# Sparse attention and two feed-forward layers: two inner slices per unit, value low halves off VectorE, one reciprocal per two pairs

## The chip, the cores and the metric

The kernel runs on one core of one Trainium2 chip. The metric is the device time of one execution in microseconds (us), the median of the runs. Five engines work side by side, each through its own instructions in order: TensorE (PE; its weight loads are listed as PEld), VectorE (DVE), ScalarE (ACT), GpSimd (POOL) and SyncE (SP, which only issues transfers here). An instruction that waits holds up all that stands behind it on its engine.

## What is computed

```python
def _attn_ref(q, k, v):                       # (4, 8, 576, 64) each
    scores = (1 / np.sqrt(D)) * np.matmul(q, k.transpose(0, 1, 3, 2))
    kth = np.partition(scores, -32, axis=-1)[..., -32:-31]
    scores = np.where(scores >= kth, scores, -1e9)
    attn = np.exp(scores - np.max(scores, axis=-1, keepdims=True))
    attn = attn / (np.sum(attn, axis=-1, keepdims=True) + 1e-9)
    return np.matmul(attn, v)
def _moe_ref(x, w_in, w_out):                 # 2304 tokens, 512 -> 2048 -> 512
    r = np.maximum(x @ w_in, 0.0)
    return (r * r) @ w_out
def _moe2_ref(x, w_skip, w_gate, w1, w2):     # 8 experts, 512 -> 1024 -> 512
    # tokens with x @ w_skip > 0 go to the expert with the largest logit:
    # x + probability * (relu(x @ w1[e]) @ w2[e]); the others stay as they are
```

All arrays are float32. The output of the attention is the input of the first feed-forward layer, and that one's output is the input of the second.

## The kernel before

Products are made in float16 with split numbers: a value is held as a high half and a low half, and three of the four products are summed. So nearly every operand is scaled, rounded to its high half, and subtracted from itself to get the low half.

**Attention.** The 18,432 rows of scores (4 batches, 8 heads, 576 rows) make 144 tiles of 128 rows by 576 columns. They are taken two at a time, in 72 ticks (`j`; `a` and `b` are the two tiles of a tick). In a tick PE makes the next pair's scores in PSUM (`qk`, tile `pS`, which has one buffer), ACT evacuates them to SBUF (`evac_s`, tile `s`), and DVE folds them into pairwise maxima and minima (`tree`, L360), finds the 32 largest values by four rounds of MAX and MATCH_REPLACE (`top32`, L379, L382) and writes a mask (`mask`, L406). ACT makes the exponentials (L401), POOL multiplies them by the mask (L415), ACT rounds them to the high half and sums the rows (`high`, L430, into `l`), POOL subtracts the low half (`low`, L435), and SP transposes both by DMA. Three ticks later PE multiplies by the values (`av`, L458), DVE has made the reciprocal of the row sums (`rinv`, L419), and ACT scales the result by it (`xout`, L476).

**Preparing q, k and v.** Raw pieces come by DMA into one of three `raw` buffers. For q and k, ACT makes the high half and a scaled copy in place, and POOL subtracts (`low_pool`). For the 32 value pieces (`vh`, 128 by 320) ACT makes the high half (L242) and DVE the low half in one instruction, with a sum for a later range check (L245, `low_dve`), placed behind `top32` and ahead of the next pair's `tree`.

**First feed-forward layer, interleaved.** When the tokens of a group are ready (a group is one token tile of 128, or two of them), `add_units` queues 16 units for it, one per slice of 128 of the inner width. A unit is: 12 matmuls into PSUM (`mm1`, L535), three ACT passes (`act1`: relu `r` L543, square `g` L545, square in float16 `gh` L547), one POOL subtraction (`g_low`, L556), and 3 matmuls per token tile (`mm2`, L568). Fourteen groups have one tile, two have two, so there are 224 units of 128 columns and 32 of 256. Each tick runs 4.4 units' worth of 128 columns, as far as units are there; the transposed tokens of a one-tile group lie in tile `xl` (shown under its tag as `xb` or `xl`), which has two buffers. What is left runs in a loop after the last tick, in which the logits, the routing (`route`), the scatters of token ids by POOL (`scatter_ids`, L837, while fewer than `DRAIN` units are left) and the split of the first 16 expert weight chunks (`next_chunk`: ACT L875, DVE L880 or POOL L877 and L878) stand among the units. The chunks' buffers lie where the attention's tiles were, so their first loads come after the last transposition of tokens.

**Second layer.** The tokens of each expert are gathered, and its blocks run one after the other.

The code gives the order of each engine only in part: a scheduler places the instructions, by priorities and dependences, when the kernel is built. The changed code therefore also stands in another order where its text is the same.

## Time and profile before

| | us |
|---|---|
| three runs | 1027.30, 1023.33, 1030.25 (median 1027.3) |
| the profiled execution | 1023.65 |
| its span, first to last instruction | 1021.8 |
| VectorE busy in the span | 845.7 (83%) |
| TensorE busy | 779.8 (76%) |
| GpSimd busy | 767.4 (75%) |
| ScalarE busy | 759.8 (74%) |

Busy times are unions over the whole span, and the span has stages that are limited by different things: the 72 ticks (to about 741 us), the loop over the units that are left (to about 833 us), and the second layer.

### The profile page before, as it was taken

The page shows a single profiled execution, that of the slowest core. Times are in us where ns is not written, and L with a number is a line of the kernel's source. Part 1 is how long each engine was busy: PE and PEld are TensorE (multiplying, and loading weights), DVE is VectorE, ACT ScalarE, POOL GpSimd, SP SyncE. Part 2 cuts the span into 40 slices and gives each one's busy share as a digit, 9 for nine tenths or more (in the row PEclk, how much of TensorE's full clock was granted, in tenths as well). Part 3 has the DMA queues.
Part 4 walks back from the last instruction along what each step waited for, and adds up shares of the span by engine and source line. Part 5 has one row for each costly group of instructions (what it writes and reads, how often), then busy time and mean ns, then how long its engine had stood idle before and what let it go on. Part 6 is the DMA issues. An engine that isn't in the chain of part 4 may idle for free. (4 is left out here: it accounts for less than half of the span.)

```text
span 1021.8 us, 25759 instructions
## 1 busy us (share of the span) xinstructions
PE 779.8 (76%) x9036; PEld 592.5 (58%) x9036; DVE 845.7 (83%) x2279; ACT 759.8 (74%) x2117; POOL 767.4 (75%) x783
## 2 busy tenths in 40 slices
PE   0123337989879979989969999999997958688852
PEld 0122226767667757667657777767775746565631
DVE  4999999999999999999989999999908634535631
ACT  7777676899988998888779989999866642544620
POOL 4576777899879898888879988899955875744850
PEclk9999999999999999999979999999998978898876
DMA  9675554668675475565475676565537508653500
GB/s 286 174 189 152 141 126 78 103 137 156 118 161 111 94 150 94 108 130 119 100 137 121 138 138 130 116 117 90 96 64 269 208 27 326 214 177 113 177 15 10
DMA packets 257023, 138.16 MB, mean 135 GB/s; under 512 B 215348, under 2 KB 238260, under 8 KB 256848
## 3 DMA queue, kind: packets, MB, share of 16 engines
q1 hardware_dynamic: 253568, 132.16, 55.7%
q0 software_dynamic: 3280, 3.80, 1.2%
q8 instruction: 94, 1.54, 0.6%
q14 instruction: 81, 0.66, 0.2%
HBM read 76.92 MB, written 7.37 MB: 82 GB/s over the span
## 5 line engine op out<-in xcount | busy, mean ns | idle before, releaser
L379 DVE MAX8 m<-tr 128x8 f32<-128x288 f32 (+1 forms) x576 | 275.8, 517 | 0.0
L435 POOL TENSOR_TENSOR phl<-e,phl 128x576 f16<-128x576 f32 x144 | 190.6, 1328 | 33.2 <-ACT phl L430 29.0
L415 POOL TENSOR_TENSOR e<-e,mk 128x576 f32<-128x576 f32 x144 | 196.0, 1371 | 21.9 <-DVE mk L406 21.9
L568 PE MATMUL px<-woh,gh 128*128 128x512 f16 x576 | 189.3, 382 | 15.9 <-POOL gh L556 10.8
L382 DVE MATCH_REPLACE8 tr<-m,tr 128x288 f32<-128x288 f32 x432 | 186.8, 437 | 0.0
L535 PEld LDWEIGHTS <-wih 128*128 128x128 f16 x2048 | 143.2, 101 | 55.4 <-issue 23.6
L535 PE MATMUL ph<-xb,wih 128*128 128x128 f16 (+1 forms) x1792 | 156.6, 231 | 21.0 <-DMA xb<-xhl 9.5
L458 PE MATMUL misc<-vh,pt 128*128 128x64 f16 (+1 forms) x2400 | 119.3, 198 | 63.7 <-ACT xn L476 33.7
L556 POOL TENSOR_TENSOR gh<-g,gh 128x128 f16<-128x128 f32 (+1 forms) x256 | 130.2, 515 | 41.1 <-ACT gh L547 27.4
L458 PEld LDWEIGHTS <-pt 128*128 128x128 f16 (+1 forms) x2400 | 100.8, 100 | 85.3 <-issue 53.2
L568 PEld LDWEIGHTS <-gh 128*128 128x128 f16 x864 | 77.5, 100 | 86.0 <-POOL gh L556 21.1
L360 DVE SCALAR_TENSOR_TENSOR tr<-pS,s 128x576 f32<-128x576 f32 x144 | 102.1, 750 | 14.8 <-ACT s L332 10.8
L401 ACT ACTIVATE e<-s,nm 128x576 f32<-128x576 f32 x144 | 111.0, 772 | 1.4 <-POOL phl L435 0.7
L568 PE MATMUL px<-wol,gh 128*128 128x512 f16 x288 | 109.7, 382 | 0.0
L430 ACT ACTIVATE phl<-e 128x577 f16<-128x577 f32 x144 | 98.0, 681 | 2.8 <-POOL e L415 2.8
L543 ACT ACTIVATE r<-ph 128x128 f32<-128x128 f32 (+1 forms) x256 | 70.3, 287 | 37.9 <-PE ph L535 36.8
L535 PE MATMUL ph<-xb,wil 128*128 128x128 f16 (+1 forms) x896 | 97.4, 230 | 0.0
L326 PE MATMUL pS<-kh,ql 128*128 128x192 f16 x576 | 67.2, 273 | 38.9 <-DMA kh<-lp 26.1
L406 DVE TENSOR_SCALAR mk<-s,m 128x576 f16<-128x576 f32 x144 | 93.3, 688 | 0.0
L545 ACT ACTIVATE g<-r 128x128 f32<-128x128 f32 (+1 forms) x256 | 82.7, 324 | 7.1 <-POOL gh L556 3.4
L332 ACT ACTIVATE s<-pS 128x1152 f32<-128x1152 f32 x72 | 80.3, 1116 | 3.7 <-PE pS L326 3.4
L547 ACT ACTIVATE gh<-r 128x128 f16<-128x128 f32 (+1 forms) x256 | 80.7, 320 | 1.3 <-PE px L568 1.0
(229 smaller groups left out, 1585.6 us busy)
## 6 DMA issues: line engine op xcount, KB each, us to landing
wraw<-in_w SPq DMA_DIRECT2D x64, 512.0 KB, 5.4
wol<-in_w_in SPq DMA_DIRECT2D x16, 512.0 KB, 4.9
raw<-in_qm SPq DMA_DIRECT2D x48, 128.0 KB, 2.8
w<-in_w_out SPq DMA_DIRECT2D x10, 512.0 KB, 3.7
raw<-in_vd SPq DMA_DIRECT2D x32, 160.0 KB, 2.8
raw<-in_kd SPq DMA_DIRECT2D x16, 288.0 KB, 3.5
out<-x SPq DMA_DIRECT2D x16, 256.0 KB, 2.6
wol<-in_w_out SPq DMA_DIRECT2D x6, 512.0 KB, 3.7
```

The costliest lines, as they stand in the source:

```text
L360: last = nc.vector.scalar_tensor_tensor(out=R2[:, :, n * 288:n * 288 + 288].rearrange("p k (c x) -> p k c x", c=3), in0=near, scalar=2.0 * ...
L379: return both(lambda k: nc.vector.max(m[k][:, 8 * r:8 * r + 8], x[k][:, :n]))
L382: both(lambda k: nc.vector.match_replace(out=dst[k][:, :n], in_to_replace=m[k][:, 8 * r:8 * r + 8], in_values=src[k][:, :n], imm_value=NEG))
L401: nc.scalar.activation(e[:, :S], st[i]["s"], AF.Exp, scale=0.125, bias=st[i]["nm"])
L406: nc.vector.tensor_scalar(out=t, in0=st[i]["s"], scalar1=st[i]["m"][:, 31:32], scalar2=None, op0=ALU.is_ge)
L415: nc.gpsimd.tensor_mul(e[:, :S], e[:, :S], st[i]["mk"])
L430: nc.scalar.activation(h[:, 0, :S + 1], st[i]["e"], AF.Copy, accum_out=st[i]["l"][:, 0:1])
L435: nc.gpsimd.tensor_sub(h[:, 1, :S], st[i]["e"][:, :S], h[:, 0, :S])
L458: nc.tensor.matmul(ps[:, a, :], lhsT=pt[:rows, 5 * low + c, :], rhs=vh[:rows, c, part * D:(part + 1) * D], start=(n == 0), stop=(n == len( ...
L535: nc.tensor.matmul(ph, lhsT=wt[:, d, u["f"] * 128:(u["f"] + 1) * 128], rhs=x[:, :, c0 + d, :], start=(n == 0), stop=(n == 11))
L556: g_last[0] = nc.gpsimd.tensor_sub(u["gh"][:, 1], u["g"], u["gh"][:, 0]).ins
L568: nc.tensor.matmul(px, lhsT=gh[:, part, t * 128:(t + 1) * 128], rhs=w[:, f, :], start=(f == 0 and n == 0), stop=(f == 15 and n == 2))
```

## The change

It has three parts.

1. A unit of a one-tile group takes two slices of the inner width: two accumulations of 12 matmuls side by side in one PSUM tile, then ACT and POOL instructions of 256 columns, then two times 3 matmuls. Such a group has 8 units and not 16. PE's matmuls stay as they were, shape by shape. `DRAIN` counts units, and is halved.
2. The low half of a value piece is made as those of q and k are: ACT scales the raw piece in place (one more pass), and POOL subtracts in its queue of low halves. The range check on those sums goes, with its four small DVE instructions.
3. The row sums of two pairs stand in one tile of 2 by 4, and every second tick makes the reciprocals of all four tiles. The reciprocal of the earlier pair is made where it was; for the later pair it is made a tick earlier relative to its use, and so it needs the row sums of the tick just before.

```diff
-DRAIN = 12
+DRAIN = 6
...
-            slot = (v_["b"] * 4 + v_["pr"]) * 2 + hd
-            low_dve.append(lambda: nc.vector.scalar_tensor_tensor(
-                out=vh[:, :, D:], in0=t3, scalar=2.0 ** V_EXP, in1=vh[:, :, 0:D],
-                op0=ALU.mult, op1=ALU.subtract, accum_out=v_low[:, slot:slot + 1]))
+            nc.scalar.activation(t, t, AF.Copy, scale=2.0 ** V_EXP)
+            low_pool.append(lambda: nc.gpsimd.tensor_sub(vh[:, :, D:], t3, vh[:, :, 0:D]))
...
-        l = apool.tile([128, 2, 2], F32, name="l", bufs=6)
+        if a % 4 == 0:
+            l4[:] = [apool.tile([128, 2, 4], F32, name="l", bufs=4)]
+        l = l4[0]
         for k in range(2):
-            st[a + k].update(m=m[:, k], nm=nm[:, k:k + 1], l=l[:, :, k])
+            st[a + k].update(m=m[:, k], nm=nm[:, k:k + 1], l=l[:, :, a % 4 + k])
...
     def rinv(a):
         l = st[a]["pair"][2]
-        nc.vector.reciprocal(l[:, 1], l[:, 0])
+        if a % 4 == 0:
+            nc.vector.reciprocal(l[:, 1], l[:, 0])
...
-            for f in range(16):
-                units.append(dict(gr=gr, f=f, n=128 * len(gr[1])))
+            step = 2 // len(gr[1])
+            for f in range(0, 16, step):
+                units.append(dict(gr=gr, fs=range(f, f + step), n=256))
...
-        ph = psum.tile([128, 256], F32, name="ph", bufs=2)[:, :u["n"]]
-        n = 0
-        for wt, c0 in ((wih, 0), (wih, 4), (wil, 0)):
-            for d in range(4):
-                nc.tensor.matmul(ph, lhsT=wt[:, d, u["f"] * 128:(u["f"] + 1) * 128], rhs=x[:, :, c0 + d, :],
-                                 start=(n == 0), stop=(n == 11))
-                n += 1
+        ph = psum.tile([128, 256], F32, name="ph", bufs=2)
+        for i, f in enumerate(u["fs"]):
+            w = 256 // len(u["fs"])
+            n = 0
+            for wt, c0 in ((wih, 0), (wih, 4), (wil, 0)):
+                for d in range(4):
+                    nc.tensor.matmul(ph[:, i * w:i * w + w], lhsT=wt[:, d, f * 128:(f + 1) * 128], rhs=x[:, :, c0 + d, :],
+                                     start=(n == 0), stop=(n == 11))
+                    n += 1
...
-            for job in low_dve:
-                with tc.issue_after(tail):
-                    tail = job().ins
-            low_dve.clear()
...
-    vl = rpool.tile([128, 4 * H], F32, name="vl")
-    nc.vector.tensor_tensor(out=vl, in0=v_low, in1=v_low, op=ALU.mult)
-    check(7, vl, 9216.0 ** 2, ALU.is_le)
```

Three places in the order show what moves. The first is DVE around a tick late in the attention (`m` the 32 values found, `tr` the folded scores, `mk` the mask). Before:

```order
L379 MAX m_10699<-tr 128x8 x2
L419 RECIPROCAL l<-l 128x2
L382 MATCH_REPLACE tr<-m_10699,tr 128x288 x2
L379 MAX m_10699<-tr 128x8 x2
L245 SCALAR_TENSOR_TENSOR vh,v_low<-raw,vh 128x5x64
L360 SCALAR_TENSOR_TENSOR tr<-pS,s 128x2x288 x2
L406 TENSOR_SCALAR mk<-s,m_10699 128x576 x2
```

After:

```order
L380 MAX m_10166<-tr 128x8 x2
L421 RECIPROCAL l<-l 128x4
L383 MATCH_REPLACE tr<-m_10166,tr 128x288 x2
L380 MAX m_10166<-tr 128x8 x2
L361 SCALAR_TENSOR_TENSOR tr<-pS,s 128x2x288 x2
L407 TENSOR_SCALAR mk<-s,m_10166 128x576 x2
```

The value's low half is gone from between the last round of MAX and the next `tree`; the reciprocal is twice as wide, and the next tick has none.

The second is ACT where the last tile of tokens is split (`xhl`), after the last tick (`r`, `g`, `gh` are the three passes of a unit, `xn` the attention's output). Before:

```order
L476 ACTIVATE xn<-misc,l 128x64 x2
L492 ACTIVATE xhl,x_sq<-xn 128x512
L493 ACTIVATE xhl<-xn 128x512
L547 ACTIVATE gh<-r 128x128 x2
L543 ACTIVATE r<-ph 128x128
L547 ACTIVATE gh<-r 128x128
```

After:

```order
L478 ACTIVATE xn<-misc,l 128x64 x2
L550 ACTIVATE g<-r 128x256
L494 ACTIVATE xhl,x_sq<-xn 128x512
L495 ACTIVATE xhl<-xn 128x512
L552 ACTIVATE gh<-r 128x256
```

The unit passes are twice as wide, and there are fewer of them left: behind the last split of `xhl` ACT still has the `r` pass of 37 units of 128 columns before, and of 15 units of 256, which is 30 of 128, after. Behind the last exponential it is 46 before and 40 after.

The third is POOL at the end of the loop over the units (the scatters of token ids are `table<-ent,sloti`). Before, a stretch of the twelve pairs of a subtraction and a scatter:

```order
L556 TENSOR_TENSOR gh<-g,gh 128x128
L837 DMA table<-ent,sloti 18432x2
L556 TENSOR_TENSOR gh<-g,gh 128x128
L837 DMA table<-ent,sloti 18432x2
L556 TENSOR_TENSOR gh<-g,gh 128x128
```

After, the first of six:

```order
L880 TENSOR_TENSOR w21l<-wraw,w21h 128x1024
L561 TENSOR_TENSOR gh<-g,gh 128x256
L839 DMA table<-ent,sloti 18432x2 x2
L561 TENSOR_TENSOR gh<-g,gh 128x256
L839 DMA table<-ent,sloti 18432x2 x2
```

As many scatters stand ahead of the last unit's subtraction as before, twelve, but two together, and between half as many subtractions.

## Rows read from the trace of the kernel before

**Rows 1.** Busy time by stage: each engine's busy us (instructions), then PEclk, DMA share, GB/s.
```profile
33.00:741.00 708.00, 566.29 (x6840) 434.65 (x6841) 697.36 (x1935) 605.60 (x1776) 598.62 (x623) 0.98 0.62 125
741.00:765.00 24.00, 24.00 (x297) 17.88 (x295) 0.45 (x5) 15.64 (x60) 12.62 (x24) 1.00 0.36 62
765.00:802.00 37.00, 29.61 (x284) 22.13 (x282) 34.13 (x108) 26.67 (x70) 22.12 (x26) 0.91 0.75 268
802.00:833.00 31.00, 26.12 (x252) 18.85 (x249) 8.55 (x31) 13.38 (x49) 26.29 (x33) 0.95 0.26 86
833.00:1022.00 189.00, 129.58 (x1350) 95.71 (x1350) 88.19 (x168) 75.60 (x120) 96.03 (x62) 0.82 0.41 142
```

**Rows 2.** Costliest groups, DVE: count, then busy us, mean ns, idle before.
```profile
L245 DVE SCALAR_TENSOR_TENSOR vh<-raw,vh 128x320 f16<-128x320 f32 x32 | 21.2, 678 | 0.0
L419 DVE RECIPROCAL l<-l 128x2 f32<-128x2 f32 x72 | 10.3, 142 | 3.8 <-ACT phl L430 3.8
L406 DVE TENSOR_SCALAR mk<-s,m 128x576 f16<-128x576 f32 x144 | 93.3, 688 | 0.0
```

**Rows 3.** Timeline of DVE in one tick: start us, us.
```profile
610.94 0.15 DVE L419 RECIPROCAL l<-l 128x2 f32<-128x2 f32 x1
611.01 0.07 DVE L382 MATCH_VALUE_LOAD tr<-m,tr 128x8 f32 x1
...
613.18 0.47 DVE L245 SCALAR_TENSOR_TENSOR vh<-raw,vh 128x320 f16<-128x320 f32 x1
...
613.58 0.75 DVE L360 SCALAR_TENSOR_TENSOR tr<-pS,s 128x576 f32<-128x576 f32 x1
```

**Rows 4.** Timeline of ACT near the same tick.
```profile
603.64 0.19 ACT L430 ACTIVATION_READ_ACCUMULATOR phl<-e 128x1 f32 x1
...
612.06 1.11 ACT L332 ACTIVATE s<-pS 128x1152 f32<-128x1152 f32 x1
```

**Rows 5.** Who waited for whom: us in total, times, longest.
```profile
DVE tr L360 <- ACT s L332: 10.8, 5, 4.3
```

**Rows 6.** Two tiles' instructions: ns min/median/max, first and last start.
```profile
L406 DVE TENSOR_SCALAR mk<-s,m x144: 500/592/1536, 34.2 to 740.0; 128x576 f16<-128x576 f32 x144
L245 DVE SCALAR_TENSOR_TENSOR vh<-raw,vh x32: 461/483/1434, 63.7 to 650.6; 128x320 f16<-128x320 f32 x32
```

**Rows 7.** Groups with shapes kept apart, ACT and POOL.
```profile
L545 ACT ACTIVATE g<-r 128x128 f32<-128x128 f32 x224 | 69.3, 310 | 6.9 <-POOL gh L556 3.4 <-ACT nm L387 0.3
L545 ACT ACTIVATE g<-r 128x256 f32<-128x256 f32 x32 | 13.5, 421 | 0.2
L242 ACT ACTIVATE vh<-raw 128x320 f16<-128x320 f32 x32 | 14.9, 466 | 15.3 <-DMA raw<-in_vd 15.2
L556 POOL TENSOR_TENSOR gh<-g,gh 128x128 f16<-128x128 f32 x224 | 108.1, 489 | 38.8 <-ACT gh L547 25.2 <-ACT g L545 5.5 <-DMA wraw<-in_w 2.2
L556 POOL TENSOR_TENSOR gh<-g,gh 128x256 f16<-128x256 f32 x32 | 22.1, 696 | 2.3 <-ACT gh L547 2.3
L222 POOL TENSOR_TENSOR ql<-raw,ql 128x256 f16<-128x256 f32 x48 | 36.9, 770 | 13.9 <-ACT raw L221 13.8
```

**Rows 8.** Timeline of POOL and SP from the last split to the first expert load.
```profile
755.30 1.16 POOL L494 TENSOR_TENSOR xhl<-xn,xhl 128x512 f16<-128x512 f32 x1 [2.98 <-ACT xhl L493]
...
761.43 1.23 SPq L500 DMA_TRANSPOSE xb<-xhl  x1
...
764.61 0.34 POOL L772 MEMSET blank<- 128x288 int32 x1 [0.94 <-DMA xb<-xhl]
```

**Rows 9.** Timeline of ACT: first and last of the first 16 chunks.
```profile
768.64 1.06 ACT L875 ACTIVATE w10h<-wraw 128x1024 f16<-128x1024 f32 x1 [1.49 <-DMA wraw<-in_w]
...
800.42 1.06 ACT L875 ACTIVATE w21h<-wraw 128x1024 f16<-128x1024 f32 x1
```

**Rows 10.** Timeline of POOL: two scatters, one unit apart.
```profile
817.08 0.99 POOL L837 DMA_INDIRECT table<-ent,sloti  x1 [0.17 <-issue]
818.71 0.99 POOL L837 DMA_INDIRECT table<-ent,sloti  x1 [0.17 <-issue]
```

More of the change, by code (lines that the diff above doesn't have):

```diff
@@ L122, in attention_two_moes @@
     lg_all = const.tile([128, NT, 9], F32, name="lg_all")
-    v_low = const.tile([128, 4 * H], F32, name="v_low")
     w_sq = const.tile([128, 20], F32, name="w_sq")
@@ L208, in new_v @@
         return apool.tile([128, 5, 2 * D], F16, name="vh", bufs=BUFS["v"])
-    low_pool, low_dve = [], []
+    low_pool = []
     def prep_piece(pc):
@@ L343, in attention_two_moes @@
     m6 = [None]
+    l4 = []
     def pair_tiles(a):
@@ L561, in mm2 @@
     def mm2(u):
-        f, gh, gr = u["f"], u["gh"], u["gr"]
-        if f == 0:
-            x2p[gr] = [psum.tile([128, DM], F32, name="px", bufs=2) for _ in gr[1]]
-        for t, px in enumerate(x2p[gr]):
-            n = 0
-            for part, w in ((0, woh), (0, wol), (1, woh)):
-                nc.tensor.matmul(px, lhsT=gh[:, part, t * 128:(t + 1) * 128], rhs=w[:, f, :],
-                                 start=(f == 0 and n == 0), stop=(f == 15 and n == 2))
-                n += 1
+        gh, gr = u["gh"], u["gr"]
+        for i, f in enumerate(u["fs"]):
+            if f == 0:
+                x2p[gr] = [psum.tile([128, DM], F32, name="px", bufs=2) for _ in gr[1]]
+            for t, px in enumerate(x2p[gr]):
+                n = 0
+                for part, w in ((0, woh), (0, wol), (1, woh)):
+                    nc.tensor.matmul(px, lhsT=gh[:, part, (t + i) * 128:(t + i + 1) * 128], rhs=w[:, f, :],
+                                     start=(f == 0 and n == 0), stop=(f == 15 and n == 2))
+                    n += 1
         if f == 15:
@@ L1187, in attention_two_moes @@
     check(6, w_abs, 2.0 ** -97, ALU.is_le)
-    vl = rpool.tile([128, 4 * H], F32, name="vl")
-    nc.vector.tensor_tensor(out=vl, in0=v_low, in1=v_low, op=ALU.mult)
-    check(7, vl, 9216.0 ** 2, ALU.is_le)
-    check(8, m31, 2.0 ** -6, ALU.is_ge)
-    nc.vector.tensor_reduce(out=good[:, 8:9], in_=good[:, 0:9], axis=AX.X, op=ALU.min)
+    check(7, m31, 2.0 ** -6, ALU.is_ge)
+    nc.vector.tensor_reduce(out=good[:, 8:9], in_=good[:, 0:8], axis=AX.X, op=ALU.min)
     cnt_f = rpool.tile([128, 8], F32, name="cnt_f")
```

## The prediction

> **What bounds the kernel now.** I read the stages first, since the four compute engines are all busy 74 to 83% of the span and a sum over it says little. In the 72 ticks, 33 to 741 us, VectorE is busy 697.4 of 708 us, while PE, ACT and POOL have 566, 606 and 599 [rows 1]: the ticks go at DVE's pace, and each microsecond off DVE there is one off the kernel, as long as the others keep up. From 741 to 765 DVE has 0.45 us of work and PE is busy all 24 us: PE works off units that have queued up, while the last pair goes through POOL, DMA, PE and ACT. From 765 to 802 DVE is again the busiest, 34.1 of 37, now with routing and the low halves of expert weights, and the units share ACT with the weight chunks. From 802 to 833 POOL (26.3 of 31) and PE (26.1) are level. The second layer, 189 us, contains nothing that the diff touches, and I move it as a block.
>
> **Part A, DVE in the ticks.** The 32 low halves took 678 ns in the mean [rows 2]. In the tick shown, the instruction took 0.47 us, but the next one began 0.40 us after it [rows 3]; instructions overlap by 0.07 us at their ends. So 32 x (0.678 - 0.07) = 19.5 us leave DVE's queue. The reciprocals read 142 ns [rows 2], but the next instruction begins 0.07 us after one [rows 3]: 36 x 0.07 = 2.5 us. Together 22.0 us. The row of 2 by 4 is not in the trace; by the row of 2 columns I take it as equal, and a size twice that would cost 36 x 0.07 = 2.5 us at the most, so the reciprocals are worth 0 to 2.5.
>
> Not all 22 can be had, since the scores run in a loop beside DVE: `tree` frees the one `pS`, PE makes the next scores, ACT evacuates them, and the next `tree` waits for that. In the tick shown the evacuation ends at 612.06 + 1.11 = 613.17 [rows 4] and `tree` starts at 613.58 [rows 3]. That is 0.41 us of slack, just what the removed instruction took. Five of the 72 trees waited already, 10.8 us in all [rows 5]. ACT gets lighter (below), which helps the loop; PE's blocks between two scores get longer, which hurts it. I take three quarters, **-16.5 us**; the ends are -8 (the loop eats most) and -24 (all of it, and 2 us of the old waits).
>
> The reciprocal's new need is the row sums of the tick before. The sum that the one at 610.94 would need [rows 3] was read at 603.64 + 0.19 = 603.83 [rows 4], 7.1 us ahead. I price that wait at nothing; the cover is those 7 us, and behind it would wait a MATCH_REPLACE and all of DVE's tick.
>
> **What ACT and POOL give and take in the ticks.** 112 pairs of narrow units become 112 wide ones. One ACT pass saves 2 x 310 - 421 = 199 ns per pair [rows 7]; with three passes of about that size, 112 x 3 x 0.199 = 67 us less on ACT, of which some 50 in the ticks. The 32 new passes over 128x320 cost what L242 does on that shape, 466 ns [rows 7], 15 us. POOL saves 112 x (2 x 489 - 696) = 31.6 us [rows 7] and gets 32 subtractions of 128x320. Their price lies between 128x256 at 770 ns [rows 7] and 128x512 at 1160 [rows 8]; in proportion 870, so 27.8 us (24.6 to 37.1). POOL ends 4 us lighter (7 lighter to 5.5 heavier), at about 599 of 708 us before. Neither sets the pace, so none of this enters the sum.
>
> That speaks against a rule of the Trainium skill: GPSIMD Engine Reference, section 4.1, sends elementwise work on two inputs to VectorE because GpSimd is about half as fast. As an estimate from that page, twice the trace's 461 ns is 0.92 us, or 29.5 us for the 32; the rows' 27.8 agree. By the rule taken alone the sum would be 16.5 us worse, without part A.
>
> More serious is that DVE and POOL get into each other's way. A mask takes 500 ns at the least, 688 in the mean, 1536 at the most; the low half 461 to 1434 [rows 2, 6]. The masks lose 144 x 188 = 27 us of DVE's time. A new subtraction could stand in a mask's way: 32 x half of 0.87 = 14 us if every one did. Against that, 112 POOL instructions disappear. I put the balance at zero, and +14 is a rival. In the Trainium skill, SBUF — State Buffer, section "Who interferes with whom", such a stall is an exclusive lock: whichever of the two starts first holds the shared ports for its whole instruction. By that rule the removed low halves also stop delaying POOL; the spread of the rows fits it.
>
> **Part B, from the last tick to the first expert load.** POOL finished the low half of the last tokens at 755.30 + 1.16 = 756.46, but their transposition was issued at 761.43, and what waits for it began at 764.61 [rows 8]. Those 4.97 us are no POOL time. The last tile's tokens need one of the two `xl` buffers; it is free when only 32 units are left to start (16 of this group and 16 of the one ahead). In the order before, 37 units' passes stand behind that split, five too many; after, 30. So the wait goes: **-4.9 us** (0 to -5). Late next is the chain through POOL itself, which is unchanged.
>
> **Part C, units among weight chunks.** Between the first and the 16th chunk on ACT lie 768.64 to 801.48 [rows 9], 32.8 us, with 15 units before and 14 after. DVE has work for 34.1 of the stage's 37 us [rows 1], so no more than 2.9 can go. A wide unit's three passes each may wait behind one more chunk, 1.06 us [rows 9]: 7 x 1.06 = 7.4 at worst. I take **-1** (-3 to +7).
>
> **Part D, the end of the loop.** There POOL alternates one scatter and one subtraction per unit: two scatters stand 818.71 - 817.08 = 1.63 us apart [rows 10]. After, two units cost 2 x 1.63 - 2 x 0.489 + 0.696 = 2.98 against 3.26, six times: 6 x 0.28 = **-1.7** (-4 to +3, since a wide unit takes longer to fill and empty the pipeline). The four check instructions that go stand beside DVE's idle time here: nothing.
>
> **Sum.** -16.5 - 4.9 - 1 - 1.7 = -24.1 us. The profiled execution took 1023.65 and becomes 999.5. It lies 3.65 us below the median of the runs, so for the median I forecast 1027.3 - 24.1 = **1003.2 us**.
>
> **Rivals.** (1) The score loop takes DVE's place: PE's longer blocks stand ahead of the next scores, the evacuation ends later, and part A keeps only a third, -7 us. For it: the 0.41 us of slack, PE at 80% in the ticks. Against: five waits in 72 so far, and the lighter ACT. 1027.3 - 7 - 4.9 - 1 - 1.7 = 1012.7. (2) The same mechanism beyond the break-even, the slower side: `tree` waits in every tick. Over the 59 ticks from 200 us on, in which units run, a mean wait of 24.1 / 59 = 0.41 us in a tick more than I allow eats the whole gain. A unit that is twice as long can cost one subtraction more on POOL before `mm2` lets PE go on, 0.70 us: 1027.3 - 24.1 + 59 x 0.70 = 1044.5. Against: the scores stand between units once a tick, in both orders, and nothing waits for them then but one block. (3) The new subtractions meet the masks: +14, so 1017.2. For it: the 27 us that masks lose now; against: POOL's instructions fall by 80. (4) More comes out of the two loops at the end: fewer hand-overs between PE, ACT and POOL let C and D reach -3 and -4, and ACT's relief lets A reach -22: 1027.3 - 22 - 4.9 - 3 - 4 = 993.4. (5) The reciprocal does wait after all, because ACT runs later: each of 36 would cost what ACT is late beyond 7.1 us. At 0.5 us each, 18 us: 1021.2.
>
> **How the numbers follow.** The forecast has 0.60, (4) 0.14, (1) 0.11, (3) 0.07, (2) 0.05, (5) 0.03. My own bounds around the forecast are 1027.3 - 24 - 5 - 3 - 4 = 991 and 1027.3 - 8 - 3 + 3 + 2 = 1021; all bad ends at once are unlikely, and I cut at the rivals (1) and (3). The range is 989 to 1016: it holds the forecast, (1) and (4), and leaves out (2), (5), most of (3) and some of the forecast's bad ends, together under 0.2. Runs of one kernel here spread over 7 us, so 1%, 10.3 us, is about what can be told from no change. Under 1017 lie nearly all of the forecast, (4), (1) and half of (3): 0.85 for faster by over 1%. Within 1%: 0.09, from the rest of (3), (5) and bad ends. Slower: 0.06, from (2) and what I have not thought of.
>
> **What would show it.** Right for A: the ticks end near 724 us instead of 741, no L245 on DVE, 36 reciprocals, DVE still busy over 98% until then, and waits of `tree` for `s` between 11 and 20 us in all. Wrong for A: those waits at 30 us or more, or the mask's mean well over 688 ns. B: the transposition is issued right behind POOL's last `xhl`, and 19 us instead of 24 lie between the last mask and the first chunk load. C and D: 36 and 29 us from there to the 16th chunk and to the routing's end. The second layer: 189 us as before; if it moves, the prediction is wrong in a place where it has no term.

## The result and the profile after

The changed kernel takes **998.2 us** in the median of 4 runs (1000.98, 995.91, 1000.52, 993.45), the kernel before 1027.3. The ratio is 0.9725, with a 95% interval of 0.9684 to 0.9765: 2.7% faster. Forecast were 1003.2 us, with a range of 989 to 1016. The profiled execution of the changed kernel took 1000.98 us, with a span of 999.1 against 1021.8: 22.7 us less, where the sum of the prediction had 24.1.

So the total is near the forecast one, but its parts are not. First the stages, by windows of the profile, with their edges at the events that stand at the edges of [rows 1]: the end of the last mask, the first expert load, the 16th weight chunk, the routing of the last tokens. Columns: length, then each engine's busy us (instructions), PEclk, DMA share, GB/s.

```profile
33.00:730.40 697.40, 572.57 (x6950) 450.47 (x6950) 689.10 (x1835) 596.52 (x1554) 613.37 (x570) 0.97 0.57 127
730.40:746.30 15.90, 15.54 (x214) 12.13 (x213) 0.18 (x1) 9.43 (x28) 9.60 (x12) 1.00 0.36 81
746.30:779.60 33.30, 27.86 (x269) 20.51 (x267) 31.00 (x96) 24.52 (x44) 18.51 (x18) 0.95 0.78 281
779.60:811.50 31.90, 27.49 (x233) 19.92 (x233) 12.45 (x41) 10.10 (x27) 24.82 (x25) 0.89 0.31 100
811.50:999.10 187.60, 126.26 (x1350) 93.13 (x1350) 89.00 (x168) 75.34 (x119) 94.88 (x62) 0.85 0.42 143
```

DVE still sets the pace of the ticks (689.1 of 697.4 us busy), and they end some 10 us earlier, not 17. PE again fills the second window. The second layer is as long as before within 1.4 us.

The groups of DVE in the ticks that answer to [rows 2], with the unit's subtraction on POOL and the fold `tr` beside them: busy us, mean ns, idle before.

```profile
L561 POOL TENSOR_TENSOR gh<-g,gh 128x256 f16<-128x256 f32 x144 | 103.9, 728 | 29.2 <-ACT gh L552 25.5
L361 DVE SCALAR_TENSOR_TENSOR tr<-pS,s 128x576 f32<-128x576 f32 x144 | 102.2, 751 | 12.7 <-ACT s L329 6.4
L407 DVE TENSOR_SCALAR mk<-s,m 128x576 f16<-128x576 f32 x144 | 104.5, 764 | 0.0
```

The low halves are gone. The masks rose from 688 ns [rows 2] to 764. By tiles, the masks (which answer to [rows 6]) and the reciprocals: ns min/median/max, first and last start.

```profile
L407 DVE TENSOR_SCALAR mk<-s,m x144: 503/700/1546, 34.8 to 729.6; 128x576 f16<-128x576 f32 x144
L421 DVE RECIPROCAL l<-l x36: 147/153/179, 75.1 to 733.5; 128x4 f32<-128x4 f32 x36
```

The fastest mask is as fast as before (503, was 500); the median went from 592 to 700. A reciprocal over 2 by 4 reads 153 ns, hardly more than the 142 of a narrow one. In the list of waits, `tree` waits for the evacuated scores less than before (10.8 us in 5 times [rows 5]):

```profile
DVE tr L361 <- ACT s L329: 6.4, 3, 3.8
```

Taken from start to start on DVE, between the first and the last mask, the 705.8 us of the kernel before become 694.8: low halves 19.5 to 0; reciprocals 4.6 to 2.7; masks 87.0 to 98.2; idle time 10.3 to 7.5; all the rest 584.4 to 586.4. So DVE lost 21.4 us of work and got 11.2 back in its masks.

Behind the ticks, POOL and SP (answering to [rows 8]): start us, us.

```profile
742.25 1.15 POOL L496 TENSOR_TENSOR xhl<-xn,xhl 128x512 f16<-128x512 f32 x1 [1.96 <-ACT xhl L495]
...
743.43 1.23 SPq L502 DMA_TRANSPOSE xb<-xhl  x1
...
746.29 0.34 POOL L774 MEMSET blank<- 128x288 int32 x1 [0.16 <-DMA xb<-xhl]
```

The split ends at 742.25 + 1.15 = 743.40 and the transposition is issued at 743.43: the wait of 4.97 us is gone. The split itself also stands nearer to the last mask: 755.30 - 740.0 = 15.3 us before [rows 6, 8], 742.25 - 729.6 = 12.65 after. The 16th chunk on ACT (answering to [rows 9]), and a stretch of the last loop on POOL (answering to [rows 10]):

```profile
778.55 1.05 ACT L877 ACTIVATE w21h<-wraw 128x1024 f16<-128x1024 f32 x1
```

```profile
791.23 0.67 POOL L561 TENSOR_TENSOR gh<-g,gh 128x256 f16<-128x256 f32 x1 [0.48 <-PE px L574]
...
796.83 0.67 POOL L561 TENSOR_TENSOR gh<-g,gh 128x256 f16<-128x256 f32 x1 [2.51 <-ACT gh L552]
...
800.11 0.67 POOL L561 TENSOR_TENSOR gh<-g,gh 128x256 f16<-128x256 f32 x1 [0.18 <-issue]
...
803.23 0.69 POOL L561 TENSOR_TENSOR gh<-g,gh 128x256 f16<-128x256 f32 x1
```

Between two wide subtractions lie 3.1 to 5.6 us, and in the longest of these steps POOL waits 2.5 us for ACT; the prediction had 2.98 for each. From the blank tile's MEMSET (746.29) to the end of the 16th chunk (779.60) are 33.3 us, 36.9 before [rows 8, 9].

### The profile page after: what moved, and what is told of

Its sections match the earlier page's. It is cut to its first block, busy times and chain, and to the rows that moved or that the text cites. A ratio compares the mean times of both kernels' runs of the same rounds, so it can differ in the third digit from the quotient of the medians.

```text
span 999.1 us, 25006 instructions
## 1 busy us (share of the span) xinstructions
PE 773.9 (77%) x9036; PEld 599.4 (60%) x9036; DVE 838.7 (84%) x2176; ACT 738.2 (74%) x1813; POOL 772.9 (77%) x703
## 5 line engine op out<-in xcount | busy, mean ns | idle before, releaser
L416 POOL TENSOR_TENSOR e<-e,mk 128x576 f32<-128x576 f32 x144 | 200.3, 1402 | 27.2 <-DVE mk L407 26.7
L574 PE MATMUL px<-woh,gh 128*128 128x512 f16 x576 | 184.3, 381 | 3.5 <-POOL gh L561 2.0
L540 PE MATMUL ph<-xb,wih 128*128 128x128 f16 (+1 forms) x1792 | 163.0, 234 | 14.2 <-DMA xb<-xhl 10.2
L574 PEld LDWEIGHTS <-gh 128*128 128x128 f16 x864 | 80.7, 99 | 83.4 <-POOL gh L561 5.4
L561 POOL TENSOR_TENSOR gh<-g,gh 128x256 f16<-128x256 f32 x144 | 103.9, 728 | 29.2 <-ACT gh L552 25.5
L407 DVE TENSOR_SCALAR mk<-s,m 128x576 f16<-128x576 f32 x144 | 104.5, 764 | 0.0
L540 PE MATMUL ph<-xb,wil 128*128 128x128 f16 (+1 forms) x896 | 99.7, 233 | 0.0
L323 PEld LDWEIGHTS <-ql 128*128 128x128 f16 x576 | 55.1, 109 | 57.3 <-ACT wih L300 17.2
L540 PEld LDWEIGHTS <-wil 128*128 128x128 f16 x1024 | 76.1, 102 | 2.5
L548 ACT ACTIVATE r<-ph 128x256 f32<-128x256 f32 x144 | 54.3, 381 | 25.1 <-PE ph L540 24.6
```

Source lines behind the costliest of these rows:

```text
L323: nc.tensor.matmul(ps[:, c], lhsT=q[:, part], rhs=kh[:, c * 192:(c + 1) * 192], start=(n == 0), stop=(n == 2 * len(jobs) - 1))
L407: nc.vector.tensor_scalar(out=t, in0=st[i]["s"], scalar1=st[i]["m"][:, 31:32], scalar2=None, op0=ALU.is_ge)
L416: nc.gpsimd.tensor_mul(e[:, :S], e[:, :S], st[i]["mk"])
L540: nc.tensor.matmul(ph[:, i * w:i * w + w], lhsT=wt[:, d, f * 128:(f + 1) * 128], rhs=x[:, :, c0 + d, :], start=(n == 0), stop=(n == 11))
L561: g_last[0] = nc.gpsimd.tensor_sub(u["gh"][:, 1], u["g"], u["gh"][:, 0]).ins
L574: nc.tensor.matmul(px, lhsT=gh[:, part, (t + i) * 128:(t + i + 1) * 128], rhs=w[:, f, :], start=(f == 0 and n == 0), stop=(f == 15 and n = ...
```

## The experiments

The theory after the result: (T) part A fell short because masks wait for POOL's instructions, above all for the new subtractions of the values; what came back behind the ticks comes from the wide units. The rivals stand in each expectation.

The three parts alone and in pairs make eight kernels, two of which were known. The other kernels change one suspected cost. This table has what the single sections draw on. "Left" counts units of 128 columns in ACT's order: behind the last exponential up to the first chunk, from there to the 16th, and after that. The three stretches go from the start of the last mask to the blank tile (which is filled when the first expert load is issued), from there to the end of the 16th chunk, and from there to the first gather of the second layer. The kernel before ran beside each series of runs, with medians of 1025.1 to 1027.3 us; the ratios are against those, so medians of different series can be compared to some 2 us.

| kernel | median us | first to last mask | last mask begins | mask mean ns | left | stretches |
|---|---|---|---|---|---|---|
| before | 1027.3 | 705.8 | 740.0 | 688 | 17, 15, 14 | 24.6, 36.9, 36.0 |
| units (E1) | 1016.9 | 714.9 | 748.1 | 707 | 12, 14, 10 | 17.1, 36.0, 30.2 |
| values (E2) | 1009.9 | 690.4 | 722.7 | 718 | 22, 15, 14 | 33.0, 35.7, 35.4 |
| reciprocals (E3) | 1018.1 | 705.6 | 738.9 | 693 | 13, 15, 14 | 18.9, 36.7, 36.3 |
| units, reciprocals (E7) | 1014.0 | 708.4 | 742.2 | 736 | 12, 14, 12 | 17.2, 32.5, 34.4 |
| values, reciprocals (E9) | 1014.2 | 686.2 | 720.5 | 724 | 22, 15, 14 | 33.2, 35.1, 35.1 |
| units, values (E12) | 1006.9 | 695.1 | 729.0 | 750 | 12, 14, 14 | 17.3, 33.5, 40.8 |
| all three (after) | 998.2 | 694.8 | 729.6 | 764 | 14, 14, 12 | 16.7, 33.3, 36.4 |
| before, three `xl` (E10) | 1025.4 | 703.9 | 737.5 | 681 | 14, 14, 18 | 19.7, 35.7, 43.6 |

### E1: the wide units alone

```diff
-DRAIN = 12
+DRAIN = 6
...
+            for f in range(0, 16, step):
+                units.append(dict(gr=gr, fs=range(f, f + step), n=256))
```

> The kernel before with the wide units alone (part 1). In the changed kernel the ticks end 10.4 us earlier and the stages after them are 12.3 us shorter (7.9, 3.6, -0.4 and 1.2). First theory: the longer masks (764 instead of 688 ns) come from the 32 new POOL subtractions of the values, and all that is won after the ticks comes from the wide units: here the masks stay at 680 to 700 ns, the last mask starts at 740 +- 2 us as before, and the time falls by 11 to 13 us, to about 1015. Rival: the wide subtractions of the units (728 ns each instead of 489) are what holds the masks up: mean 740 ns or more here, the last mask near 748, and a fall of 5 us at most.

Measured: 1016.9 us, ratio 0.990 (0.9858 to 0.9941). The last mask began at 748.1 us, 8.1 later than before, and the masks rose by only 19 ns. Neither expectation is met: the total is the first theory's, the last mask's time the rival's. From the first to the last mask the kernel took 9.1 us more: masks 2.5, the old low halves 2.5 (756 in place of 678 ns), idle time 4.5. All that the wide units gain, and these 8 us too, comes out behind the ticks, in the first and the third stretch.

### E2: the values' low halves alone

```diff
-            low_dve.append(lambda: nc.vector.scalar_tensor_tensor(
...
+            nc.scalar.activation(t, t, AF.Copy, scale=2.0 ** V_EXP)
+            low_pool.append(lambda: nc.gpsimd.tensor_sub(vh[:, :, D:], t3, vh[:, :, 0:D]))
```

> The kernel before with the change of the values' low halves alone (part 2). First theory: the removed instructions give DVE 19.5 us and the masks take 8 to 11 of them back (mean 750 to 765 ns); the last mask starts 8 to 11 us earlier than in the kernel before, the stages after the ticks stay as they were, and the time is about 1017. Rival (the wide units' subtractions hold the masks up): masks near 690 ns, the last one 17 to 19 us earlier, time about 1008. A third way: ACT (15 us more) and POOL (28 us more) with narrow units become too slow for DVE's pace, and the ticks gain less than 6 us while waits of `tree` for `s` exceed 15 us.

Measured: 1009.9 us, 0.9825 (0.980 to 0.9849). The last mask began 17.3 us earlier, as the rival had it, and the masks took 4.4 us back, half of what the theory had. Neither had the stretch behind it: 33.0 us from the last mask to the first load, 8.4 more than before, since the order leaves 22 units there and not 17.

### E3: the reciprocals alone

```diff
+        if a % 4 == 0:
+            l4[:] = [apool.tile([128, 2, 4], F32, name="l", bufs=4)]
...
+        if a % 4 == 0:
+            nc.vector.reciprocal(l[:, 1], l[:, 0])
```

> The kernel before with the reciprocals once per two pairs alone (part 3). Prediction's term: 36 x 0.07 = 2.5 us less on DVE, 0 if the one of 2 by 4 takes twice as long; its rows in the changed kernel read 153 ns, so about 2.5 us. Whatever holds the masks up, their mean stays within 10 ns of 688. The time lies between -3 and 0 us of the kernel before, which 3 rounds can hardly tell from no change; the start of the last mask, 2 to 3 us earlier, is the better reading.

Measured: 1018.1 us, 0.9911 (0.9888 to 0.9935). The masks did as expected (693 ns), and the last began 1.1 us earlier. But the kernel gained 8.5 us in the median (1026.6 in this series) and 5.1 in the spans, where the reciprocals in DVE's queue fell by 1.9 (4.6 to 2.7). The first stretch alone is 5.7 us shorter: the order leaves 13 units there in place of 17. I had not foreseen that.

### E4: the changed kernel without POOL's new subtractions

```diff
-            nc.scalar.activation(t, t, AF.Copy, scale=2.0 ** V_EXP)
-            low_pool.append(lambda: nc.gpsimd.tensor_sub(vh[:, :, D:], t3, vh[:, :, 0:D]))
+            nc.scalar.activation(vh[:, :, D:], t3, AF.Copy, scale=0.0)
```

> The changed kernel without POOL's 32 subtractions for the values' low halves: ACT fills those halves with zeros in the pass that scaled the raw piece in place, so the low half of the values is left out of the result and ACT has as many passes as in the changed kernel. First theory (these subtractions hold the masks up): the masks fall back to 680 to 700 ns, the last mask starts 9 to 11 us earlier than in the changed kernel (near 719), time about 10 us below it, near 988. Rival (the wide units' subtractions): masks stay at 750 ns or more, and the time is within 3 us of the changed kernel's 998. A second rival: masks are held up whenever DVE's tick is shorter, since POOL's unchanged work then fills more of it; then they stay above 720 ns and the gain is below 6 us.

Measured: 995.3 us, 0.9682 (0.9657 to 0.9707), 3 us below the changed kernel. The masks fell to 709 ns, which is 8.4 us of DVE's queue, and the last one began at 723.7, 5.9 us earlier. This lies between the theory (9 to 11) and its rivals. The new subtractions are a part of the cause, not the whole of it. They do little of it by standing in a mask's way themselves: in the changed kernel 4 masks begin while one of them runs, and lose 1.8 us. The rest of the 8.4 us is lost beside other POOL instructions, which lie elsewhere without them; the order differs too (12, 16 and 10 units left for 14, 14 and 12).

### E5 and E6: masks that never wait

```diff
-        t = apool.tile([128, S], F16, name="mk", bufs=2)
-        nc.vector.tensor_scalar(out=t, in0=st[i]["s"], scalar1=...
+        t = apool.tile([128, 3, 200], F16, name="mk", bufs=2)[:, :, :192]
+        nc.vector.tensor_scalar(out=t, in0=st[i]["s"].rearrange("p (c x) -> p c x", c=3), scalar1=...
```

> The changed kernel with the mask written into a tile of three rows of 192 with gaps of 8 (the input and POOL's multiplication seen as three rows too). Theory (the mask needs something that POOL's two-input instructions hold, because it runs at 500 ns for 576 columns, nearly two columns per ns-pair of the other passes, whose fastest over 576 take 742 ns): with rows that can't be cut into two equal halves it runs at one column a step, 640 to 680 ns at the least, but waits for nobody: mean within 20 ns of the minimum, POOL's multiplication back from 1402 to about 1290 ns. Ticks about 10 us shorter (764 -> 670 ns, 144 times, less the 0.08 overlap either way). In the order 32 units are left behind the last exponential and not 40, so the end shrinks by up to 8 x 1.4 us more. Time 975 to 990. Rival (masks are long for another reason, such as a wait for the row of values or for a free tile): minimum 640 or more and the same 260 ns on top, mean near 900, ticks 20 us longer. Rival 2: the gaps change nothing (minimum 500, mean 764), only the order's smaller backlog shows: -5 to -11 us.

> The kernel before with the same gaps in the mask. Theory: masks go from 500 to 1536 (mean 688) to 640 to 680 without spread: -1 to -6 us for DVE's ticks. In the order 42 units and not 46 are left behind the last exponential, 34 behind the last split, as in the kernel with the reciprocals alone, where the end shrank by 5.7 us: together 1015 to 1021. Rival (another reason): mean near 850 ns and 1040 us or more.

Measured: 1021.3 us (E5, on the changed kernel, 23 us above it) and 1048.5 (E6, on the kernel before; ratio 1.0177, 1.0113 to 1.024). Both totals miss what was expected. POOL's multiplication in these two kernels reads its tiles as the same three rows. The masks of E5 by tile, and beside them POOL's multiplication from the page and the wait of `tree`:

```profile
L407 DVE TENSOR_SCALAR mk<-s,m x144: 798/804/822, 33.9 to 750.3; 128x576 f16<-128x576 f32 x144
```

```profile
L417 POOL TENSOR_TENSOR e<-e,mk 128x576 f32<-128x576 f32 x144 | 186.7, 1311 | 8.4 <-DVE mk L407 8.3
```

```profile
DVE tr L361 <- ACT s L329: 22.3, 16, 3.6
```

This is the clearest reading of the study. In the gapped form all 144 masks take between 798 and 822 ns, though 97 of them begin while a POOL instruction runs, and POOL is busy for 591.5 of the 718 us from 33 to 751 (82%, against 88% in the changed kernel). The flat ones take from 503 to 1546.

The trace also shows what a slow mask waits for. Here is one of the changed kernel, with the POOL instruction that runs as it begins:

```profile
444.69 0.89 POOL L561 TENSOR_TENSOR gh<-g,gh 128x256 f16<-128x256 f32 x1
...
444.97 0.93 DVE L407 TENSOR_SCALAR mk<-s,m 128x576 f16<-128x576 f32 x1
```

POOL's instruction ends at 445.58, the mask at 445.90, 0.32 us later. It is so with every one of them. In the changed kernel 65 masks take 503 to 531 ns, and each of the other 79 ends 312 to 321 ns after a POOL instruction does. In the kernel before these are 74 masks and 314 to 322 ns, and 15 of the 32 low halves end 347 to 353 ns after one. The holding up goes both ways. In the changed kernel 25 of POOL's wide subtractions begin while a mask runs, and take 860 ns in the mean; beside the gapped masks of E5, 28 do, and take 674. POOL's multiplications fell from 1402 to 1311 ns in the mean with the same shortest one (1271 and 1269), so it is not their changed form that shortens them.

So the masks' extra time is waiting for POOL's instructions, and only the fast form waits. By the Trainium skill, SBUF — State Buffer, section "Who interferes with whom", DVE and GpSimd exclude each other on a shared pair of ports. The trace agrees: a slow mask ends at a fixed distance from the end of POOL's instruction. By the Trainium skill, VectorE: DVE Perf Modes, section "Mode 2×_2P — use both read ports for one tensor", a one-source pass can read through both ports when its outermost dimension is even, or odd and the same in input and output. The trace fits a gapped pass that can't: it takes 804 - 503 = 301 ns more, and no longer waits. No run shows whether its input, which has no gaps, counts as one row, as that rule would need here.

What I had wrong was the price: 804 ns, not 640 to 680, more than the 764 of a mask with its waits. And `tree` now waits for `s` 22.3 us in E5 and 26.8 in E6. That is most of E5's loss: from the first to the last mask E5 takes 21.6 us more than the changed kernel, 4.7 in masks and 19.8 in idle time, with 2.9 less elsewhere. The order also places the units otherwise (256 before the last mask in E5, 250 in the changed kernel); whether that or the longer masks make the wait was not separated. TensorE's granted clock was 0.91 in E5's ticks and 0.97 in the changed kernel's; E5's ten runs, at 0.894 to 0.929 over the span, do not get shorter with a higher one.

### E7 and E9: the changed kernel without one part

E7 leaves the values' low halves on DVE (parts 1 and 3), E9 keeps narrow units (parts 2 and 3).

```diff
-    low_pool = []
+    low_pool, low_dve = [], []
...
+                out=vh[:, :, D:], in0=t3, scalar=2.0 ** V_EXP, in1=vh[:, :, 0:D],
```

> The changed kernel with the values' low halves on DVE as in the kernel before (parts 1 and 3). By the parts alone the ticks should be 7 to 8 us longer than in the kernel before (wide units +9.1, reciprocals -0.2 in the profiles), with masks near 707 ns; the end shrinks as in the wide units alone, since the order leaves 38 units behind the last exponential and 30 behind the last split. Time 1013 to 1018. If the parts aren't additive in the ticks and the wide units cost nothing there with the lighter reciprocals, 1005 to 1010.

```diff
-DRAIN = 6
+DRAIN = 12
...
-            for f in range(0, 16, step):
-                units.append(dict(gr=gr, fs=range(f, f + step), n=256))
+            for f in range(16):
+                units.append(dict(gr=gr, f=f, n=128 * len(gr[1])))
```

> The changed kernel with the narrow units of the kernel before (parts 2 and 3). By the runs so far the wide units cost 3 to 9 us in the ticks (longer subtractions for the masks to meet) and give back more behind them, because the order then leaves fewer units between the last exponential and the first weight chunk: here it leaves 22 (of 128 columns), 17 in the kernel before, 14 in the changed one. At 1.45 us of PE each (24.6 us for 17 in the kernel before) that is 31 to 33 us from the last mask to the first chunk load, 16.7 in the changed kernel. So: last mask at 719 to 723 us, masks at 700 to 720 ns, and 1007 to 1012 us in all. Rival: the shorter passes, not the number of units left, make the end short; then narrow units with this order give 24 us there as in the kernel before, and about 1000 us.

Measured: E7 1014.0 us, 0.9864 (0.9815 to 0.9912), as expected in the total; the ticks were only 2.6 us longer and the masks higher (736 ns) than expected. E9 1014.2, 0.9879 (0.9853 to 0.9906): the last mask at 720.5 and 33.2 us behind it are as expected, masks at 724 ns a little higher, the total 2 us above the range. The rival of E9 is out: the first stretch is long again with narrow units, 33.2 us for 22 units, while the reciprocals alone, narrow too, had 18.9 for 13. It is above all the number left that counts. Width counts beside it: 14 units left take 16.7 us in the changed kernel and 19.7, as narrow ones, in E10.

E9 is also part A as the prediction had it, without the wide units: the stretch from the first to the last mask falls by 19.6 us. The wide units on top of it take 8.6 back, 6.0 of them in masks (92.2 to 98.2 us). Counted by the POOL instruction that runs as a mask begins, units' subtractions meet 41 masks in E9 and cost them 5.7 us, and 32 and 10.6 us with wide units.

### E8: narrow subtractions in the changed kernel

```diff
-            g_last[0] = nc.gpsimd.tensor_sub(u["gh"][:, 1], u["g"], u["gh"][:, 0]).ins
+            for c in (0, 128):
+                g_last[0] = nc.gpsimd.tensor_sub(u["gh"][:, 1, c:c + 128], u["g"][:, c:c + 128],
+                                                 u["gh"][:, 0, c:c + 128]).ins
```

> The changed kernel with POOL's subtraction of a unit made in two halves of 128 columns; ACT and PE keep the wide units. In the changed kernel 33 masks begin while a unit's subtraction runs and lose 11.1 us there, 336 ns each; in the kernel before 38 lose 6.5, 171 ns each. If the length of the instruction that is met is what costs, the loss there falls to 5 to 7 us and the masks' mean to 720 to 740 ns; POOL pays 144 x (2 x 0.47 - 0.70) = 35 us, most of it within its idle 12%, so the time is within -4 and +8 us of the changed kernel. If the masks lose no less (over 10 us there), it is not the length but how often POOL is busy.

Measured: 1002.2 us, 0.9747 (0.9691 to 0.9803). For each mask I took the POOL instruction under way when it began, and its time over 505 ns. Units' subtractions met 38 masks before and cost them 6.5 us (171 ns each), 32 and 10.6 us after (332 each; the expectation counts one more), 41 and 7.9 us here (193 each). So the length of what is met is the price, as expected. The mean did not fall, though; it rose to 794 ns, since 35 masks met `phl`'s subtractions here and lost 18.2 us, and 16 lost 9.1 in the changed kernel. In all, 104 masks begin beside a POOL instruction here and 84 in the changed kernel, with POOL busy for 91% of the ticks in place of 88. What a mask is spared at one instruction it meets in another.

### E10: a third buffer for the tokens, in the kernel before

```diff
-... tag="xb" if len(gr[1]) == 2 else "xl", bufs=2)
+... tag="xb" if len(gr[1]) == 2 else "xl", bufs=2 if len(gr[1]) == 2 else 3)
```

> The kernel before with three buffers for the tokens of one-tile groups in place of two. Prediction's part B: the 4.97 us between POOL's last split and the transposition are a wait for such a buffer, so here the transposition follows at once and the stretch from the last mask to the first chunk load falls from 24.6 to 19 to 20.5 us. In the order the units between the last exponential and the first chunk fall from 17 to 14, and those behind the 16th chunk rise from 14 to 18. If the later loops hide units, the kernel gains 4 to 5 us (about 1022). If the last loop costs 1.63 us for each of the four, as its scatters stood, the gain is given back: 1026 +- 2.

Measured: 1025.4 us, 0.9987 (0.9967 to 1.0008): no change that can be told. POOL and SP behind the last mask:

```profile
752.93 1.16 POOL L494 TENSOR_TENSOR xhl<-xn,xhl 128x512 f16<-128x512 f32 x1 [2.98 <-ACT xhl L493]
```

```profile
754.12 1.23 SPq L500 DMA_TRANSPOSE xb<-xhl  x1
```

The split ends at 754.09 and the transposition follows at 754.12. The stretch falls from 24.6 to 19.7 us, just what part B had. And the gain is given back: the order now leaves 18 units and not 14 for the last loop, and it takes 43.6 us in place of 36.0, 1.9 us for each. Removing the wait alone is worth nothing. A wait for a buffer that units free is the units' time under another name.

### E11: mask and multiplication in one pass of DVE

```diff
-        nc.vector.tensor_scalar(out=t, in0=st[i]["s"], scalar1=st[i]["m"][:, 31:32], scalar2=None, op0=ALU.is_ge)
+        nc.vector.scalar_tensor_tensor(out=e[:, :S], in0=st[i]["s"], scalar=st[i]["m"][:, 31:32], in1=e[:, :S],
+                                       op0=ALU.is_ge, op1=ALU.mult)
...
-            apply_mask(pa)
-            apply_mask(pb)
```

> The changed kernel with mask and multiplication as one DVE pass (row of scores not below the 32nd value, times the exponentials), both exponentials of a pair ahead of it, and four tiles for them in place of three. POOL loses 144 multiplications, 200 us. DVE's pass reads two tiles; the nearest row is the conversion over 128x512, 668 ns at the least, so 735 to 755 over 576, 0.67 in the queue against 0.686 for a mask now with its waits. Theory (the masks lose time to POOL's instructions, so the less POOL is busy, the less they lose): POOL is some 60% busy in the ticks and not 88; the pass loses 100 to 160 ns in the mean (mean 850 to 900 ns, since a pass over two tiles also meets POOL), so DVE's ticks get 10 to 20 us longer by that, while what waited for POOL (26.7 us before the multiplications, ACT and PE behind it) goes: 1000 to 1015 us. Rival: the waits vanish with POOL's load far below its present one: mean under 780 ns, the ticks as long as now or up to 8 us shorter, the order leaves 36 units and not 40 behind the last exponential, and the time is 985 to 996. A second rival: exponentials come too late for DVE, which now waits for them at each tick's end: 1020 or more, with the wait named in the chain of waits.

Measured: 1026.9 us, 0.999 (0.9962 to 1.0017), 29 us above the changed kernel. The total is that of the second rival, without its reason: DVE waits for the exponentials 3.6 us in all. The pass by tile, and the ticks by windows:

```profile
L407 DVE SCALAR_TENSOR_TENSOR e<-s,m,e x144: 802/814/1832, 32.7 to 757.0; 128x576 f32<-128x576 f32 x144
```

```profile
33.00:757.00 724.00, 586.95 (x7041) 458.94 (x7039) 707.09 (x1832) 603.27 (x1557) 432.20 (x431) 0.93 0.53 123
```

POOL is 60% busy (432.2 of 724), as expected, and the pass loses 958 - 802 = 156 ns in the mean, within the expected 100 to 160. What I had wrong is again the price of the undisturbed pass, 802 ns in place of 735 to 755. From the first to the last mask the kernel takes 29.6 us more than the changed one: 27.4 in these passes, 9.4 in idle time, and 7 less elsewhere. Unlike the gapped mask the pass has a spread (to 1832 ns). It meets POOL's instructions too: 90 passes take 802 to 843 ns, and each of the other 54 ends 610 to 617 ns after a POOL instruction does.

### E12: the changed kernel with a reciprocal per pair

```diff
-        if a % 4 == 0:
-            nc.vector.reciprocal(l[:, 1], l[:, 0])
+        nc.vector.reciprocal(l[:, 1], l[:, 0])
```

> The changed kernel with a reciprocal per pair, as in the kernel before (parts 1 and 2). In all kernels so far the time from the last mask to the first gather of the second layer goes with the units that the order leaves behind the last exponential: 103.4 to 104.1 us for 51 units, 97.5 to 99 for 46, 89.9 to 91.9 for 42, 83.5 to 85.2 for 38, 83.3 for 36, some 1.57 us a unit. Here the order leaves 40, as in the changed kernel, which took 86.4: so 85 to 88 us here. The ticks: 36 reciprocals more, 1.9 us by the queue's rows, so the last mask at 731 to 733 us. Together 999 to 1003 us. Rival: the alone-kernel's -8.5 us was the reciprocals' own doing and not the order's; then this kernel loses them, 1005 to 1008 us.

Measured: 1006.9 us, 0.9829 (0.9789 to 0.9869). The total is the rival's; its reason does not hold. The last mask began at 729.0, no later than in the changed kernel, so 36 reciprocals cost the ticks nothing that can be seen. The end took 91.6 us where I expected 85 to 88. The place is the last loop: 40.8 us with 14 units, 36.4 with 12. My rule of a total of units left was too simple: where they are left counts. In the last loop wide kernels took 30.1 to 30.3 us for 10 (E1, E4 and E8), 34.4 and 36.4 for 12, and 40.8 for 14, some 2.6 us for 128 columns; narrow ones 34.9 to 36.3 for 14 and 43.6 for 18, some 1.9. Below that it hardly gets shorter: 27.3 us for 6 in E11, 28.0 for 4 in E5. So these are prices of the last units only. Why the order leaves fewer units at the end when there are fewer reciprocals stays open.

## Why the prediction was right in the total, and where it was not

**Part A, forecast -16.5, measured -10.4** (740.0 to 729.6 for the last mask). The working of the queue was right: 22.0 us were to leave DVE's queue, and 21.4 left it. The step that failed is "I put the balance at zero", on DVE and POOL in each other's way; the masks took 11.2 us. The prediction had the mechanism, as rival (3), but only part of its cause: it looked at the new subtractions and set 80 POOL instructions fewer against them. The number of meetings did not change: 83 masks began beside a POOL instruction before and 84 after. What a mask lost in one did. Over 505 ns, by the instruction that ran as the mask began, all masks lost 26.3 us before and 37.3 after. Of these 11 us more, the values' new subtractions have 1.8, the units' subtractions 4.1 (6.5 to 10.6), the low halves `phl` 2.9 (6.2 to 9.1) and the multiplications 3.1 (none to 3.1); the others lost 0.9 less.

The experiments say the same by parts. The values' part raises the masks by 4.4 us on the kernel before (E2), and without its subtractions the changed kernel's are 8.4 lower (E4). The wide units raise them by 2.5 on the kernel before (E1) and by 6.0 on top of the other two (after against E9), where fewer subtractions that are 1.5 times as long take twice as much from a mask. The parts don't add up. POOL's share of busy time does not tell the loss either: E9 has 90% and masks of 724 ns, the changed kernel 88% and 764. By its own test, "wrong for A if the mask's mean is well over 688 ns", part A was wrong; the size of rival (3) came, 11.2 of its 14 us, but mostly not by the new subtractions that it named.

The other step of A was too careful: a quarter was held back for the score loop, and the loop took nothing. `tree` waited 6.4 us in place of 10.8, where 11 to 20 were forecast. Rivals (1) and (2) are out. So is (5): the reciprocal of 2 by 4 is no longer than priced, and it hardly waits.

**ACT and POOL "none of this enters the sum"** holds for ACT, which is busy for 596.5 us of the ticks in place of 605.6 [rows 1]. For POOL it was the same mistake as the balance: its time was not on the path, but in the way of it. Nor did POOL end 4 us lighter there; it is busy for 613.4 us in place of 598.6. The prices were good: 728 ns in the mean for the wide subtraction, where 696 was used, and 27.7 us for the 32 new ones, where 27.8 was. But the 31.6 us that the wide units save were counted over the whole kernel, and within the ticks it is 17.4 (105.3 to 87.9); besides, the multiplications took 4.4 us longer.

**Part B, forecast -4.9, measured -7.9** (24.6 to 16.7). The wait for `xl` went, as forecast, for 4.9. Besides, the chain through POOL, which I had called unchanged, begins 2.7 us earlier; that fewer units stand ahead of the last products on PE fits this, but no run separates it. E10 says how to read B: that the wait was for a buffer is shown, since a third one ends it, but removing it alone is worth nothing. So B is worth what it is because fewer units are left in the stretch (17 to 14) without more being left behind it.

**Part C, forecast -1, measured -3.6** (36.9 to 33.3), within its bounds; its size is not explained further, and E1 and E8 had no such gain (36.0 and 36.2).

**Part D, forecast -1.7, measured +0.4** (36.0 to 36.4 to the first gather). The term was "two units cost 2.98 against 3.26". By the slopes between the kernels a wide unit costs 5.2 us in that loop, two narrow ones 3.8 (E12). In the stretch shown POOL waits for ACT in between, up to 2.5 us, which the sum of POOL's own instructions does not hold. That there are 12 to do and not 14 pays for it.

**The rest**, which I moved as a block, is 1.2 us shorter in these two profiles. Together: -10.4 - 7.9 - 3.6 + 0.4 - 1.2 = -22.7 us. The forecast of -24.1 came out by luck: 6 us too much in the ticks met 5 us too little behind them. In the medians the kernel gained 29.1 us. The 6.4 us between that and -22.7 is only where the two profiled executions lie among their runs: 3.65 below the median before, 2.8 above it after. Rival (4) had a surplus at the end, in C and D and beside an A of -22; of these only C came.

What the prediction did not weigh at all is that each part changes the order that the scheduler makes, and with it how many units are left where. The reciprocals show it best. They are worth 1.9 us on their engine. By the table they give the kernel 9.2 us alone, 2.9 beside the wide units and 8.7 beside both other parts (E3, E7, E12), and beside the values alone they cost it 4.3 (E9 against E2). The wide units are worth 3.0 to 16.0 us in the same way, the values 3.9 to 17.4. So no part has a worth of its own, and the total of -29.1 can't be shared out among the three.

## What to carry to other kernels

Where two engines hold each other up, an instruction that moves to the idler one, or grows there, is not free because that engine has time: look at the spread (min, median, max) of the busier engine's instructions, and price what is added by the length of what will be met. Whether such a spread is the other engine's doing shows when the ends are lined up: here every slow mask ended a fixed time after an instruction of POOL. Where a scheduler places the work, count in the order, before and after, how much of the filler work is left at each stage's end; that number, at a price per unit read from the stage, told more here than the instructions that were edited. And a wait that the filler work ends is not gained by removing it alone, since the filler still has to run. A change that moves such an order has to be tried beside the others, since what it gives alone, here 9.2 us, may be a loss of 4.3 in other company.

## What the runs showed of the hardware

- A one-source pass of DVE over 576 columns, f32 to f16, takes 495 to 505 ns at the least in the eleven kernels that have it, and up to 1689 (E8) beside POOL's work. Written to three rows of 192 with gaps, it takes 795 to 822 in all 288 cases (E5, E6). The slow form would be the better one only where the fast one loses 300 ns in the mean; here it lost 181 (E10) to 290 (E8).
- In these eleven kernels 834 such passes take over 565 ns, and every one of them ends 312 to 323 ns after a two-input instruction of POOL does.
- A two-source pass over 576 columns takes 802 ns at the least, as much as the gapped one-source pass, and has the spread of the fast form (to 1832 ns) with POOL 60% busy. Its 54 slow cases end 610 to 617 ns after a POOL instruction (E11).
- A reciprocal over 128x4 reads 153 ns, over 128x2 142 [rows 2].
